# A wait ahead of the bursts of a row transform, five groups in flight in the next stage with six buffers, and a weight load in four pieces

## The chip, the cores and the metric

The kernel runs on one core of one Trainium2 chip. Its time is the device time of one execution in microseconds (us). The kernel before takes 1448.63 us, the median of three runs (1447.44 to 1449.13). The profile comes from one further execution of 1447.48 us, in which the span from the first to the last instruction is 1445.7 us.

## The reference

Two results over 2048 tokens with 576 channels are mixed by a gate per token.

```python
g = sigmoid((x * gate_w).sum(-1))
# a: a state-space layer as a long convolution
K = einsum("dn,dnl,dn->dl", C, exp(dt*A*l), dt*B).real      # 576 x 2048 taps from 128 states
y = irfft(rfft(u, 2L) * rfft(K, 2L))[:L] + u * Dskip
# b: a product-key mixture of 4096 single-neuron experts, 32 heads
q = einsum("nd,dhc->nhc", x, w_q)                           # two halves of 128 per head
s1, s2 = q1 . k1, q2 . k2                                   # 64 scores each; best 2 of each
top_s, top_e = best 2 of the 4 sums
out = sum over 64 picks of softmax(top_s) * gelu(x . u[e]) * v[e]
result = g * a + (1 - g) * b
```

The kernel computes x.u for all 4096 experts as a dense product, and the weighted sum of v as a dense product with a sparse matrix. Each number of a product is split into a high and a low 16-bit part, so that a product takes three passes.

## The kernel before, in words

**Who sets the order.** The kernel text is a planner. While it emits instructions it keeps a clock of its own, with assumed costs for each engine (classes `Engine`, function `mm`, `dma`), and runs some forty coroutines from a heap. A coroutine yields a time, or yields until a tile is due by that clock (`ready`), a bank of PSUM is free (`need`) or a slot is free. Whatever is emitted first stands first on its engine. So an edit of a few lines can move instructions on all engines behind it. The chip follows the order alone and waits by semaphores; the planner's times are not times of the chip.

**Row halves.** A matmul whose contraction has 64 rows uses one half of TensorE's rows. `rows` queues a product as 13 or 14 matmuls for the upper half and as many for the lower half; `row_slot` emits one matmul for each half in turn, out of `upper` (the queue of upper halves) and `lower`. While both are filled, the two halves work at the same time. `upper` is empty for a moment when one product's upper part has been emitted and the next is not yet begun.

**The stages.** In the first stage (to about 690 us) TensorE computes the scores (tiles `s`, weights `whl`/`wrem` folded from `wq` and the keys, tile `wb`) and the dense x.u (tiles `a`), both in row halves, and in between pieces of the convolution. The generator of the taps makes phases (`kP`), exponentials and sines, and a burst of 128 small matmuls for every second chunk (`kb`, 18 bursts); its coroutine `k_gen` already waits up to 6 planner us for `upper` to be empty. `u_stage1` transforms the input u in 16 rounds `p`; each has two bursts (`hh`) of six matmuls of 288 columns (tiles `u1_p_g_hh`, weights `tu`, data `uh`), and stores its result through `us` to DRAM. While such a round runs, `hungry` may be set, which keeps `k_front` from taking a bank for the next phases.

In the second stage, `k_stage1` transforms the taps: 32 groups `w` of eight matmuls of 288 columns (tiles `k1_w_hh`, data `ksb`) in row halves between the scores, each group in two banks of the set `wb` of four. ScalarE or VectorE copies a group into a buffer `k1o`, and SyncE's queue stores that to DRAM (`sk_d<-k1o`, 288 KB). `ring(n)` lets n groups be begun and not yet stored in the planner's account. In the same stretch `v_norm` loads the rows of u for the gate (`vn`, four transfers of 72 KB a tile); GpSimd multiplies and ScalarE sums them (`vj`). `w_next` loads the last weights of the scores, `wq`, 1152 KB for half of one of eight parts. Nearly all transfers are issued in order on SyncE's queue (SP).

In the third stage (`products`) the two spectra are multiplied and transformed back (`pr`, `pi`, `pv`). Then come one-hot matrices, the sparse matrix (`S`, `gl`, `wh`) and the last product with v (`o`), to the end.

Of the kernel before, what the change touches and what calls it, by code (L numbers as in the profile page):

```python
# [13 lines left out]
F32 = mybir.dt.float32  # L14
# [11 lines left out]
D = 576  # L26
# [6 lines left out]
NCK = 144 // NI  # L33
# [107 lines left out]
def body(ctx: ExitStack, tc: tile.TileContext, xT, au, par, logdt, dskip, gatew, wq, kT, uT, vv,  # L141
# [5 lines left out]
    clock = [0.0]  # L147
# [11 lines left out]
    def key(x):  # L159
        n = x.tensor.name  # L160
        return (n, x.offset) if n in columns else n

    def size(x):
        n = 1
        for d in x.shape[1:]:
            n *= d
        return n
# [34 lines left out]
    def dma(o, i, q=None):  # L202
        t = max(clock[0], rdy.get(key(i), 0.0), queue[0])
        queue[0] = t + 0.45
        wire[0] = max(wire[0], t) + (2 if o.dtype in (F16, BF16) else 4) * o.shape[0] * size(o) / 3.4e5
        rdy[key(o)] = max(rdy.get(key(o), 0.0), wire[0] + 2.2)
        (q or DQ).dma_start(o, i)
# [10 lines left out]
    upper, lower = deque(), []  # L218
# [71 lines left out]
    def ready(*xs, late=0.0):  # L290
        while True:
            t = max(rdy.get(key(x), 0.0) for x in xs) + late - clock[0]
            if t <= 0:
                return
            yield t
# [32 lines left out]
    def need(tag, n=1):  # L328
        while tag in banksets:
            lst = sorted(vacant)  # L330
            if held[tag] + n <= caps[tag] and len(lst) >= n and lst[n - 1][0] <= clock[0]:
                return
            yield max(0.2, min(0.3, lst[n - 1][0] - clock[0])) if len(lst) >= n else 0.3
        while True:
            lst = sorted(slots[tag])
            if len(lst) >= n and lst[n - 1] <= clock[0]:
                return
            yield max(0.2, lst[n - 1] - clock[0]) if len(lst) >= n else 0.3

    def take(tag, name):  # L340
        lst = slots[tag]
        assert lst, name
        lst.remove(min(lst))
# [52 lines left out]
    def pair_rows(x, n):  # L396

        return bass.AP(tensor=x.tensor, offset=x.offset + n * R1 * D, ap=[[D, R1], [32 * R1 * D, 4], [1, D]])
# [26 lines left out]
    def root_scale(bound2, margin, again=False):  # L425

        c, h, a, b = (newcol(again) for _ in range(4))
        V.tensor_scalar(sc[:, c], bound2, margin, 2.0 ** -120, op0=OP.mult, op1=OP.max)
        V.tensor_scalar(sci[:, h], sc[:, c].bitcast(I32), 24, 23, op0=OP.logical_shift_right, op1=OP.logical_shift_left)
        V.tensor_scalar(sci[:, a], sci[:, h], -1.0, float(204 << 23), op0=OP.mult, op1=OP.add)  # L430
        V.tensor_scalar(sci[:, b], sci[:, h], float(50 << 23), None, op0=OP.add)
        return sci[:, a].bitcast(F32), sci[:, b].bitcast(F32)
# [32 lines left out]
    def slot(shape, dt, name):  # L465
        take("slot", name)
        return bp.tile([128] + shape, dt, tag="s", name=name, bufs=9)
# [10 lines left out]
    def copy(o, i):  # L478
        copy2(((o, i),))
# [163 lines left out]
    whl, wl, sk, halves, scaled = {}, {}, [], {}, []  # L643
    side = lambda: "kb" if caps["wb"] == 0 else "wb"

    def w_load(c, h):
        a = slot([4, D], F32, f"wq{c}_{h}")
        g = 8 * c + 4 * h
        dma(a, wq[:, g:g + 4, :])
        wl[c, h] = a  # L650
# [94 lines left out]
    def w_next(c, h):  # L745
        while sdone[0] < c - (kdone[0] == NCK) and 8 * NT - len(groups) < NT * c - 5:
            yield 0.3
        yield from need("raw")
        take("raw", "raw")
        yield from need("slot")  # L750
        w_load(c, h)
        yield from w_half(c, h, wl[c, h])

    def w_build(c):
# [8 lines left out]
    kdone, kstored = [0], [0]  # L763
# [423 lines left out]
    def ring(n):  # L1187

        state = [0, set()]

        def enter():
            while state[0] - len(state[1]) >= n:
                yield 0.3
            state[0] += 1

        return enter, lambda k: state[1].add(k), lambda: len(state[1])

    def u_stage1():
        nonlocal uf
        yield from need("slot")  # L1200
        us = slot([4, D], F32, "us")
        columns.add(us.tensor.name)
        s_u, i_u = root_scale(nx2, 1.02)
        ended = [0]
        ld = {}

        def load(p):
            a = us[:, p % 2, :]
            for g in range(2):
                l, far = U_PAIRS[2 * p + g]  # L1210
                dma(a[64 * g:64 * g + 64], bass.AP(tensor=au.tensor, offset=au.offset + l * D,
                                                   ap=[[64 * D, R1], [(far - l) * D, 2], [1, D]]))
            tu = uf.tile([128, 2, 128], F16, tag="tu", name=f"tu{p}", bufs=2)
            dma(tu, tu_d[:, p])
            ld[p] = a, tu

        def tail(p, hh, tag, pbs):
            for g in range(2):
                o = us[:, 2 + g, :]
                pb = pbs[g]  # L1220
                yield from ready(pb)
                ov = o[:, 288 * hh:288 * hh + 288]
                S.activation(ov, pb[:, :288], AF.Copy)
                free(tag, ov, of=pb)
                if hh:
                    yield from ready(ov)
                    dma(pair_rows(su_d, 2 * p + g), o)
            ended[0] += hh

        load(0)  # L1230
        for p in range(NT):
            a, tu = ld.pop(p)
            yield from ready(a, tu)
            while ended[0] < p - 1:
                yield 0.3
            h = uf.tile([128, 2, D], F16, tag="uh", name=f"uh{p}", bufs=1)
            S.activation(h[:, 0], a, AF.Copy, scale=s_u)
            yield from ready(h)
            V.scalar_tensor_tensor(h[:, 1], a, s_u, h[:, 0], op0=OP.mult, op1=OP.subtract)
            if p + 1 < NT:  # L1240
                load(p + 1)
            yield from ready(h)
            while ended[0] < p:
                yield 0.3
            tag = side()
            hungry[0] = p * NCK < 17 * kdone[0]
            for hh in range(2):
                yield from need(tag, 2)
                pbs = [bank(tag, f"u1_{p}_{g}_{hh}") for g in range(2)]
                cs = slice(288 * hh, 288 * hh + 288)  # L1250
                for n, (z, w) in enumerate(((0, 0), (0, 1), (1, 0))):
                    for g in range(2):
                        r = slice(64 * g, 64 * g + 64)
                        mm(pbs[g][:, :288], tu[r, z], h[r, w, cs], n == 0, n == 2, 0.063)
                spawn(tail(p, hh, tag, pbs))
                del pbs
            hungry[0] = False
            yield 12
        while ended[0] < NT:
            yield 1  # L1260
        free("slot")
        quota(raw=2)
        while not kstored[0]:
            yield 1
        V.scalar_tensor_tensor(iuk, iuk, 2.0 ** -28, i_u, op0=OP.mult, op1=OP.mult)
        UF.__exit__(None, None, None)
        uf = 0

    def k_stage1(ksb, fk, tabs):
        enter, leave, count = ring(3)  # L1270

        def tail(w, o, pbs, gs):
            while not all(g["done"] for g in gs):
                yield 0.2
            yield from ready(*pbs)
            for hh in range(2):
                copy(o[:, 288 * hh:288 * hh + 288], pbs[hh][:, :288])
                free("wb", o, of=pbs[hh])
            yield from ready(o)
            dma(pair_rows(sk_d, w), o)  # L1280
            leave(w)

        for w in range(32):
            tkt = tabs[w // 16]
            yield from ready(tkt, ksb)
            yield from enter()
            o = fk.tile([128, D], F32, tag="s1o", name=f"k1o{w}", bufs=4)
            pbs, gs = [], []
            yield from need("wb", 2)
            for hh in range(2):  # L1290
                pb = bank("wb", f"k1_{w}_{hh}")
                pbs.append(pb)
                gs.append(rows(*([(pb[:, :288], tkt[h:h + 64, w % 16, n],
                                   ksb[h:h + 64, 2 * hh:2 * hh + 2, :, w, :].rearrange("p j c i -> p (j c) i"),
                                   h == 0 and n == 0, h == 64 and n == 1) for n in range(2)] for h in (0, 64)), first=True))
            spawn(tail(w, o, pbs, gs))
            del pb, pbs
        while count() < 32:
            yield 0.5
# [634 lines left out]
    while groups or acts:  # L1934
# [5 lines left out]
        a = choose(acts, a_fit)  # L1940
# [29 lines left out]
    for t in ORDER:  # L1970
        until(lambda: t in st)
        h = st.pop(t)
# [70 lines left out]
```

## Time and profile before

| what | us |
|---|---|
| median of three runs | 1448.63 |
| the profiled execution | 1447.48 |
| its span | 1445.7 |
| TensorE (PE) busy in the span | 1420.3 |
| VectorE (DVE) busy | 1199.7 |
| ScalarE (ACT) busy | 836.9 |
| GpSimd (POOL) busy | 470.1 |

The profile has a page with shares, a view by stretches of time, a view of who waited for whom, the chain of work that ended last, and the instructions in order of time. Busy time of PE counts a matmul in one row half as fully as two side by side. In the order of time, rows that follow each other with equal text are merged: the first number is the start, the second the length of the merged piece, and in brackets stands the idle time before it with what ended it.

### The profile page before, as it was taken

The page shows a single profiled execution, that of the slowest core. Times are in us where ns is not written, and L with a number is a line of the kernel's source. Part 1 is how long each engine was busy: PE and PEld are TensorE (multiplying, and loading weights), DVE is VectorE, ACT ScalarE, POOL GpSimd, SP SyncE. Part 2 cuts the span into 40 slices and gives each one's busy share as a digit, 9 for nine tenths or more (in the row PEclk, how much of TensorE's full clock was granted, in tenths as well). Part 3 has the DMA queues.
Part 4 walks back from the last instruction along what each step waited for, and adds up shares of the span by engine and source line. Part 5 has one row for each costly group of instructions (what it writes and reads, how often), then busy time and mean ns, then how long its engine had stood idle before and what let it go on. Part 6 is the DMA issues. An engine that isn't in the chain of part 4 may idle for free. (4 is left out here: it accounts for less than half of the span.)

```text
span 1445.7 us, 43987 instructions
## 1 busy us (share of the span) xinstructions
PE 1420.3 (98%) x17652; PEld 888.2 (61%) x17654; DVE 1199.7 (83%) x4611; ACT 836.9 (58%) x1454; POOL 470.1 (33%) x484
## 2 busy tenths in 40 slices
PE   7999999999999999999799999999999999999998
PEld 3465555554654654555565444446888888788887
DVE  5887687989988979789688998589989889889770
ACT  6547878778779688595576665655423322323230
POOL 0443273563553626631255899800000000000000
PEclk9999999999999999999999999999999999999999
DMA  9333543342351241236767689778334332531410
GB/s 316 118 109 98 170 135 121 93 141 84 114 173 67 76 122 46 86 114 221 225 226 248 230 283 325 248 236 280 120 120 126 129 120 76 178 121 68 137 59 17
DMA packets 134381, 215.89 MB, mean 149 GB/s; under 512 B 10913, under 2 KB 79905, under 8 KB 127777
## 3 DMA queue, kind: packets, MB, share of 16 engines
q1 hardware_dynamic: 134080, 213.01, 45.3%
q8 instruction: 138, 2.26, 0.7%
q14 instruction: 67, 0.54, 0.1%
q10 hardware_dynamic: 96, 0.07, 0.0%
HBM read 141.74 MB, written 71.30 MB: 147 GB/s over the span
## 5 line engine op out<-in xcount | busy, mean ns | idle before, releaser
L216 PE MATMUL s<-whl,xb 64*128 64x512 f16 x3072 | 478.7, 377 | 0.3 <-ACT k1o L136 0.3
L216 PE MATMUL a<-xb,uhl 64*128 64x512 f16 (+1 forms) x3024 | 470.0, 376 | 1.3 <-DVE CS L136 0.6
L216 PE MATMUL o<-vhl,wh 128*128 128x288 f16 x3072 | 387.3, 286 | 0.0
L216 PEld LDWEIGHTS <-wh 128*128 128x128 f16 x3072 | 295.8, 98 | 76.6 <-issue 4.1
L216 PEld LDWEIGHTS <-xb 64*128 64x128 f16 x3456 | 224.3, 94 | 178.4 <-issue 15.5
L216 PEld LDWEIGHTS <-uhl 64*128 64x128 f16 (+1 forms) x3024 | 194.6, 94 | 166.4 <-issue 10.0
L136 ACT ACTIVATE wh<-gl,s_wg 128x1024 f16<-128x1024 f32 x64 | 68.9, 1137 | 188.9 <-DVE gl L136 188.9
L136 POOL TENSOR_TENSOR CS<-CS,ex 128x512 f32<-128x512 f32 x72 | 91.7, 1306 | 161.6 <-DVE ex L136 145.2
L136 DVE FIND_INDEX8 i<-m,sx 128x8 uint32<-128x64 f32 x648 | 127.8, 218 | 0.0
L136 DVE TENSOR_TENSOR gl<-S,gl 128x256 f32<-128x256 f32 x256 | 90.7, 414 | 42.9 <-PE S L216 29.8
L216 PE MATMUL s<-wrem,xb 64*128 64x512 f16 x384 | 123.1, 376 | 0.0
L216 PE MATMUL a<-xb,wrem 64*128 64x512 f16 (+1 forms) x380 | 121.9, 376 | 0.0
L136 POOL TENSOR_TENSOR e<-aN,rt 128x512 f32<-128x512 f32 x72 | 84.0, 1186 | 62.2 <-PE kb L216 62.2
L136 ACT ACTIVATE gl<-gl 128x1024 f32<-128x1024 f32 x64 | 63.8, 1048 | 66.6 <-DMA gl<-g_d 66.6
L136 ACT ACTIVATE go<-a,i_a 128x512 f32<-128x512 f32 x100 | 68.1, 684 | 57.0 <-PE a L216 38.8
L136 DVE MAX8 m<-sx 128x8 f32<-128x64 f32 x648 | 89.2, 209 | 8.6 <-ACT sx L136 8.4
L136 DVE TENSOR_TENSOR Bg<-Be,vals 128x1024 f16<-128x1024 f16 x128 | 82.8, 688 | 2.2
L136 DVE SCALAR_TENSOR_TENSOR wh<-gl,s_wg,wh 128x1024 f16<-128x1024 f32 x64 | 78.9, 1277 | 1.0 <-ACT wh L136 0.9
L136 DVE TENSOR_TENSOR A<-iota_a,vals 128x2048 f16<-128x2048 f16 x64 | 77.7, 1214 | 0.0
L136 ACT ACTIVATE CS<-CS 128x1024 f32<-128x1024 f32 x69 | 71.2, 1050 | 9.5 <-DVE CS L136 9.3
L136 DVE FIND_INDEX8 i<-m,s 128x8 uint32<-128x64 f32 x376 | 75.7, 219 | 0.0
L216 PEld LDWEIGHTS <-A 128*128 128x128 f16 x2048 | 70.1, 97 | 5.7 <-issue 1.1
(208 smaller groups left out, 2355.9 us busy)
## 6 DMA issues: line engine op xcount, KB each, us to landing
g_d<-go SPq DMA_DIRECT2D x128, 256.0 KB, 2.7
gl<-g_d SPq DMA_DIRECT2D x32, 1024.0 KB, 6.7
wq<-in_wq_dram SPq DMA_DIRECT2D x16, 1152.0 KB, 6.2
su_d<-us SPq DMA_DIRECT2D x32, 288.0 KB, 2.6
sk_d<-k1o SPq DMA_DIRECT2D x32, 288.0 KB, 2.9
vn<-in_vv_dram SPq DMA_DIRECT2D x32, 288.0 KB, 4.8
ui<-su_d SPq DMA_DIRECT2D x16, 576.0 KB, 4.7
ki<-sk_d SPq DMA_DIRECT2D x16, 576.0 KB, 5.7
```

The lines of the kernel that those rows point to most:

```text
L136: return f(*a, **k)
L216: return T.matmul(o, l, r, start=start, stop=stop)
```

## The change

Three edits. `w_next` loads `wq` in one transfer while chunks of taps are still to be made, and afterwards in four of 288 KB, 2 planner us apart. `u_stage1` waits, ahead of each of its two bursts of a round, until `upper` is empty, though at most 2 planner us. `k_stage1` lets five groups be in flight, not three, and has six buffers `k1o`, not four.

```diff
@@ w_next
         yield from need("slot")
-        w_load(c, h)
+        a = wl[c, h] = slot([4, D], F32, f"wq{c}_{h}")
+        if kdone[0] < NCK:
+            dma(a, wq[:, 8 * c + 4 * h:8 * c + 4 * h + 4, :])
+        else:
+            for j in range(4):
+                dma(a[:, j], wq[:, 8 * c + 4 * h + j, :])
+                yield 2.0
         yield from w_half(c, h, wl[c, h])
@@ u_stage1
             hungry[0] = p * NCK < 17 * kdone[0]
             for hh in range(2):
+                end = clock[0] + 2
+                while upper and clock[0] < end:
+                    yield 0.1
                 yield from need(tag, 2)
@@ k_stage1
-        enter, leave, count = ring(3)
+        enter, leave, count = ring(5)
...
-            o = fk.tile([128, D], F32, tag="s1o", name=f"k1o{w}", bufs=4)
+            o = fk.tile([128, D], F32, tag="s1o", name=f"k1o{w}", bufs=6)
```

What this makes of the order is seen at two places. The first is TensorE at the first burst of round 11 of `u_stage1` (tiles `s2_8`, `s2_12`, `s2_13` are scores in row halves, `xb` their weights). Before:

```order
L216 LDWEIGHTS xb2_535
L216 MATMUL s2_8_6054<-whl2_4551,xb2_535 128x512
L216 LDWEIGHTS xb3_619
L216 MATMUL s2_12_6006<-whl2_4551,xb3_619 128x512
L216 LDWEIGHTS tu11_5519
L216 MATMUL u1_11_0_0_6076<-uh11_5805,tu11_5519 128x288
```

After:

```order
L216 LDWEIGHTS wb4_4954
L216 MATMUL kP17_1_6000<-rt_356,wb4_4954 128x512
L216 LDWEIGHTS xb3_619
L216 MATMUL s2_13_6004<-whl2_4437,xb3_619 128x512
L216 LDWEIGHTS xb3_619
L216 MATMUL s2_13_6004<-whl2_4437,xb3_619 128x512
```

Before, two products stand there in turn, one in each half. After, the burst has moved behind a row of twelve matmuls of one product, `s2_13`, all for the upper half, of which the first two are shown; ahead of `kP17_1` stand thirteen of another, `a3_2_0`, all for the lower half.

The second place is SyncE's queue in the middle of the second stage (`vn` are the rows for the gate). Before:

```order
L207 DMA sk_d_67<-k1o3_12163 32x4x576
L207 DMA wq7_0_12320<-in_wq_dram 128x2304
L207 DMA sk_d_67<-k1o6_12293 32x4x576
L207 DMA vn37_12386<-in_au_dram 32x576 x4
L207 DMA sk_d_67<-k1o5_12219 32x4x576
L207 DMA sk_d_67<-k1o7_12312 32x4x576
L207 DMA sk_d_67<-k1o8_12381 32x4x576
```

After:

```order
L207 DMA sk_d_67<-k1o13_12456 32x4x576
L207 DMA wq7_0_12613<-in_wq_dram 128x576
L207 DMA sk_d_67<-k1o15_12543 32x4x576
L207 DMA wq7_0_12613<-in_wq_dram 128x576
L207 DMA vn41_12676<-in_au_dram 32x576 x4
L207 DMA sk_d_67<-k1o16_12587 32x4x576
L207 DMA wq7_0_12613<-in_wq_dram 128x576
L207 DMA sk_d_67<-k1o17_12607 32x4x576
L207 DMA vn42_12769<-in_au_dram 32x576 x4
L207 DMA wq7_0_12613<-in_wq_dram 128x576
```

The one load of 1152 KB between the stores of groups 3 and 6 has become four loads of 288 KB between those of groups 13 and 18.

## The prediction

> **What bounds the kernel now.** First the page, for the shares:
>
> ```profile
> span 1445.7 us, 43987 instructions
> PE 1420.3 (98%) x17652; PEld 888.2 (61%) x17654; DVE 1199.7 (83%) x4611; ACT 836.9 (58%) x1454; POOL 470.1 (33%) x484
> ```
>
> TensorE (PE) is busy for 98% of the span. Then the view by stretches (length, busy time of PE, PEld, DVE, ACT, POOL, granted clock, DMA share, GB/s), cut at the stages, and the last step of the chain that ended last:
>
> ```profile
> 12.00:690.00 678.00, 675.10 (x8858) 367.76 (x8860) 577.01 (x2771) 508.96 (x830) 293.90 (x238) 1.00 0.40 125
> 697.00:720.50 23.50, 18.52 (x200) 13.02 (x199) 15.78 (x111) 14.67 (x44) 10.41 (x17) 1.00 0.58 183
> 720.50:727.30 6.80, 4.45 (x30) 3.20 (x31) 2.78 (x7) 3.11 (x7) 1.41 (x1) 0.50 0.90 309
> 727.30:785.00 57.70, 56.75 (x667) 36.04 (x667) 54.31 (x368) 40.18 (x117) 29.41 (x62) 1.00 0.68 223
> 785.00:942.00 157.00, 156.15 (x2040) 75.01 (x2034) 126.75 (x611) 95.12 (x262) 134.77 (x162) 1.00 0.79 271
> 942.00:1023.00 81.00, 80.97 (x934) 49.41 (x931) 77.22 (x126) 43.76 (x57) 0.00 (x0) 1.00 0.78 250
> 1023.00:1442.00 419.00, 418.93 (x4820) 338.70 (x4819) 337.71 (x563) 122.43 (x123) 0.00 (x0) 1.00 0.32 105
> 1397.96 44.11 PE o L216 x360
> ```
>
> PE has no idle time to speak of except between 697 and 727 us, the front of the taps' transform: 23.50 - 18.52 = 5.0 us idle, then 6.80 us at half clock of which 2.35 us idle. Behind 1023 us PE is the chain. In 942 to 1023 us the chain runs over DVE, but PE is as full (80.97 of 81.00). So I count in PE time: what is taken off PE's work or its idle time shortens the run, what is added lengthens it.
>
> Who PE waited for, in 12 to 690 us (the first two rows) and in 697 to 785 us (the rest; total, times, longest):
>
> ```profile
> PE u L216 <- DVE uh L136: 0.6, 1, 0.6
> PE u L216 <- DVE CS L136: 0.3, 1, 0.3
> PE k L216 <- DVE k1o L136: 5.0, 2, 4.1
> PE k L216 <- ACT k1o L136: 2.5, 2, 1.3
> PE k L216 <- DMA vn<-in_au_dram: 0.5, 1, 0.5
> PE s L216 <- ACT k1o L136: 0.3, 1, 0.3
> ```
>
> The second stage holds 8.3 us of waits, half of it one wait of 4.1. In order of time, on PE, DVE and SyncE's queue (SPq), with the two medians from issue to landing:
>
> ```profile
> 718.09 0.64 PE L216 MATMUL s<-whl,xb 64*128 64x512 f16 x3
> 722.85 0.39 PE L216 MATMUL k<-ksb,tk 64*128 64x288 f16 x1 [4.12 <-DVE k1o L136]
> 722.34 0.82 DVE L136 COPY k1o<-k 128x288 f32<-128x288 f32 x2 [6.71 <-DMA sk_d<-k1o]
> 711.47 1.95 SPq L207 DMA_DIRECT2D vn<-in_au_dram  x4
> 713.51 0.52 SPq L207 DMA_DIRECT2D sk_d<-k1o  x1
> 714.14 0.53 SPq L207 DMA_DIRECT2D wq<-in_wq_dram  x1
> 714.76 0.52 SPq L207 DMA_DIRECT2D sk_d<-k1o  x1
> 715.38 2.47 SPq L207 DMA_DIRECT2D vn<-in_au_dram  x4
> 717.95 2.93 SPq L207 DMA_DIRECT2D sk_d<-k1o  x3
> wq<-in_wq_dram SPq DMA_DIRECT2D x16, 1152.0 KB, 6.2
> sk_d<-k1o SPq DMA_DIRECT2D x32, 288.0 KB, 2.9
> ```
>
> At 714.14 the 1152 KB of `wq` are issued, and the stores of `k1o` come behind. DVE wants a buffer whose store has not landed and stands still for 6.71 us; nobody empties the banks; PE runs dry at 718.73 and goes on at 722.85. The clock falls to 0.50 from 720.5 to 727.3, so the work from 722.85 to 727.3 (4.45 us) takes twice its time: 2.2 us lost.
>
> **The change part by part.** *The stall.* With six buffers a copy needs the store of the sixth group back, not the fourth, and the 1152 KB no longer stand in one piece ahead of the stores. I take the wait away whole: -4.1 us, and with it the half clock, -2.2 us. The other waits of the stage (8.3 - 4.1 = 4.2 us) hang on banks and on ScalarE, which the change leaves: 0.
>
> *What comes late next.* The order now has a quick run, from group 13 to group 25. Between the stores of these two stand on SP 11 stores, 4 pieces of `wq` and 4 tiles `vn` of four transfers. From the starts above a store takes 714.76 to 715.38 = 0.62 us of the queue, `wq` as much, a tile `vn` 711.47 to 713.51 = 2.04: 11 x 0.62 + 4 x 0.62 + 4 x 2.04 = 17.5 us. On PE the same piece is 64 matmuls of 512 columns and 88 of 288, priced by these rows:
>
> ```profile
> 703.77 0.69 PE L216 MATMUL k<-ksb,tk 64*128 64x288 f16 x8
> 704.26 0.85 PE L216 MATMUL s<-whl,xb 64*128 64x512 f16 x6
> 974.63 2.11 PE L216 MATMUL a<-xb,uhl 64*128 64x512 f16 x18
> 976.57 0.38 PE L216 MATMUL a<-xb,wrem 64*128 64x512 f16 x1
> 129.00 0.81 PE L216 MATMUL a<-xb,uhl 64*128 64x512 f16 x3
> 129.65 0.59 PE L216 MATMUL a<-xb,wrem 64*128 64x512 f16 x2
> ```
>
> Eight of 288 in 0.49 us are 0.061 each; 18 of 512 in 1.94 us are 0.108 each, when both halves are filled. That makes 64 x 0.108 + 88 x 0.061 = 12.3 us, some 1.0 a group; with the pieces where one half is alone nearer 14, 1.15 a group. The queue falls 3.5 to 5.2 us behind by the end; a store needs 0.5 + 2.9 us more to land; the buffer comes round after six groups, 6.2 to 6.9 us. So a wait comes back of 0 (3.5 + 3.4 against 6.9) to 2.4 us (5.2 + 3.4 against 6.2). I take 1.0, nearer the low end, because some of these transfers can use the queue's gaps ahead of the run: +1.0.
>
> *The order of the row halves.* The last two rows above show a half alone: three matmuls from 129.00 to 129.65, 0.216 us each, twice the 0.108. Each matmul of 512 that runs alone so costs 0.108 us. I stepped through PE's two orders, put each matmul on its half, and counted, between changes of tile size, the columns for which the other half has nothing, in units of 512. If PE takes matmuls strictly in order there are 218 before and 272 now; if it may begin up to five ahead, fewer in both, and 42 to 49 more now. The new ones lie in the first stage: 12 and 11 around round 11 of `u_stage1`, and about 11 and 10 ahead of round 15. The wait alone does not make them: one half runs out when no product can be begun. So +4.5 (42 x 0.108) to +5.8 us (54); I take 48, +5.2.
>
> *The bursts of u.* The two waits at them, 0.6 and 0.3 us, may be covered by the added 2 us: between 0 and -0.9; I take -0.5. Behind the waiting coroutine stands the next round's load only; `k_front` is held longer by `hungry`, which is in the count above.
>
> *The pieces of `wq`.* Four halves (`wq6_0` to `wq7_1` in SP's order) are now four pieces each: 12 more issues of 0.62 us on SP, hidden where that queue has gaps, and counted above where it has not. The pieces land later than the whole did:
>
> ```profile
> vn<-in_vv_dram SPq DMA_DIRECT2D x32, 288.0 KB, 4.8
> ACT wj L136 <- DMA wq<-in_wq_dram: 1.3, 1, 1.3
> ```
>
> From the first piece to the last the queue issues three stores, two tiles `vn` and four pieces, 7.0 us or so; with 4.8 us to land (the like size from the like side) the half is there after 11.8 us instead of 6.2, 5.6 later. Only ScalarE waited for `wq` here, 1.3 us, and PE has other products: 0, with 5.6 as the far end. The Trainium skill speaks against this edit: "DMA: Bandwidth & Descriptors", section "Bandwidth", says to batch transfers to 1 MiB or more. By its fit in "Anatomy of one DMA" (2.0 us and the bytes at 436 GB/s, for the other issue path) the whole would take an estimated 4.7 us and four pieces one by one 10.7. The trace has 6.2 for the whole under load, and no piece of 288 KB of `wq`.
>
> **Sum**, against the profiled execution: 1447.48 - 4.1 - 2.2 + 1.0 + 5.2 - 0.5 = 1446.9 us. That execution lies 1.15 us below the median of the runs, so I say 1448.0 us: no difference that a measurement of this kernel tells from no change, which is about 0.2% or 2.9 us.
>
> **Rivals.** *The stall comes back in the quick run* (slower). The place is the copies of groups 24 and 25. The queue also stands still itself where a `vn` buffer is not free, and then the whole old price returns, 4.1 + 2.2 us instead of the 1.0: 1448.0 + 5.3 = 1453.3. It decides from about 2 us of further delay of the queue, since that makes a PE wait of 3 us and more, and the clock fell within 1.8 us of such a wait. For it speaks the 17.5 against 12.3 to 14 us; against it that the run is short and slow pieces follow.
>
> *All waits of the second stage go* (faster). Two of the other waits are banks that ScalarE empties late because it stands behind `vj`:
>
> ```profile
> ACT vj L136 <- POOL vn L136: 10.9, 7, 3.1
> ```
>
> In SP's order the load of `wq6_1`, which stood between the four parts of `ksb`, now stands behind them, so that `ksb`, `vn` and `vj` can come sooner. Then 4.2 and the 1.0 go as well: 1448.0 - 5.2 = 1442.8. Against it: the `vn` loads themselves are as before.
>
> *The split weights are late* (slower). If PE runs out of products before the last part of the scores, it waits up to the 5.6 us: 1453.6. By the page named above this is how it would go; the order has other products there, so I give it little.
>
> *The edit in `u_stage1` does not do what it says*: in round 11 the burst still stands beside an upper half, since 2 us ran out first. That is part of the likeliest case.
>
> **How the numbers follow.** No difference: 0.44. All waits go: 0.26. The stall comes back: 0.24; late weights: 0.06. So faster 0.26, same 0.44, slower 0.30. The likeliest case has its own range by the ends of its terms: 1447.48 - 6.3 + 0 + 4.5 - 0.9 + 1.15 = 1445.9 to 1447.48 - 6.3 + 2.4 + 5.8 - 0 + 1.15 = 1450.5. The range that is to hold 8 in 10 reaches to the other cases, 1442.8 to 1453.6.
>
> **What would show it.** The view of waits: no `PE k <- DVE k1o` over 2 us, and no half clock between 690 and 800 us. In 12 to 690 us, about 5 us more until the last `kb` for the same products, with rows like `s x11` that start 0.216 apart at round 11. A half clock in the second stage, or waits there over 6 us in sum, would speak for the slower rival; an `s` that waits for `whl` for the late weights. I would be wrong altogether if the order elsewhere brings new waits of more than 3 us, which I can't see from it.

## The result, and the profile after

The changed kernel takes 1455.51 us, the median of six runs (1454.69 to 1457.08), beside 1447.43 us for the kernel before on the same chip. The ratio is 1.0054 with the interval 1.0044 to 1.0064: half a per cent slower. Forecast were 1448.0 us and no difference, with a range that ended at 1453.6. The profiled execution is the quickest of the six, 1454.69 us.

The page of the kernel after, its first lines:

```profile
span 1452.9 us, 43977 instructions
PE 1428.6 (98%) x17652; PEld 890.6 (61%) x17654; DVE 1188.4 (82%) x4598; ACT 839.5 (58%) x1457; POOL 468.5 (32%) x484
```

TensorE (PE) has as many instructions as before, and is busy 8.3 us longer (1428.6 against 1420.3). The view by stretches of the kernel after:

```profile
12.00:690.00 678.00, 674.47 (x8694) 366.08 (x8696) 557.98 (x2642) 504.37 (x818) 291.60 (x238) 0.99 0.39 122
363.18:370.01 6.83, 6.77 (x34) 3.06 (x34) 6.22 (x9) 3.40 (x8) 5.58 (x5) 0.50 0.27 77
697.00:785.00 88.00, 80.31 (x997) 52.05 (x995) 76.31 (x525) 56.58 (x165) 39.31 (x75) 1.00 0.79 256
785.00:942.00 157.00, 156.94 (x2033) 75.68 (x2031) 130.56 (x701) 97.81 (x274) 137.35 (x168) 1.00 0.75 260
```

The last step of its chain:

```profile
1405.08 44.11 PE o L216 x360
```

The same stretch of the second stage in the kernel before:

```profile
697.00:785.00 88.00, 79.72 (x895) 52.26 (x897) 72.87 (x485) 57.96 (x168) 41.23 (x80) 0.96 0.67 219
```

Three things are to be read. In 12 to 690 us PE finishes 8694 matmuls where it finished 8858, though it is as busy (674.47 against 675.10): its work goes more slowly. (Of the 164 fewer, 81 are of 512 columns, 8.7 us at 0.108; most of the others are small ones, done later.) There is a new stretch at half clock in the first stage, 363.18 to 370.01 us. And the second stage has lost its half clock (1.00 against 0.96), but not its idle time: 88.00 - 80.31 = 7.69 us after, 88.00 - 79.72 = 8.28 before.

That gives the sum. The last row of the chain ends at 1405.08 + 44.11 = 1449.19 us, 7.1 us later than before (1442.07). Idle time of PE: first stage 3.53 after, 2.90 before, +0.6; second stage -0.6; third 0.06 against 0.85, -0.8. Half clock: half of the 6.77 us of busy time in it, 3.4, against 2.2 before, +1.2. What is left, 7.1 - 0.6 + 0.6 + 0.8 - 1.2 = 6.7 us, is work that went more slowly at full clock. I put it down to matmuls of one row half with nothing beside them; a difference that is left over doesn't show that by itself, so a count of them stands beside it further down.

Who PE waited for, in 12 to 690 us (first two rows) and in 697 to 785 us:

```profile
PE kP L216 <- DVE ko L136: 1.1, 1, 1.1
PE u L216 <- DVE CS L136: 0.3, 1, 0.3
PE k L216 <- DMA ksb<-k_d: 2.3, 1, 2.3
PE wn L216 <- ACT wj L136: 1.9, 3, 0.9
PE s L216 <- ACT k1o L136: 1.7, 2, 1.4
PE k L216 <- ACT sx L136: 1.0, 1, 1.0
```

The wait of 4.1 us on a copy of VectorE (DVE) is gone. In its place stand four that were not there or were shorter: on the data `ksb` at the front of the stage, on ScalarE's pieces of the weights (`wj`), on its copies `k1o` and on `sx`.

In order of time, PE at round 11 of `u_stage1`:

```profile
356.85 2.76 PE L216 MATMUL a<-xb,uhl 64*128 64x512 f16 x12
359.45 0.38 PE L216 MATMUL a<-xb,wrem 64*128 64x512 f16 x1
360.95 0.82 PE L216 MATMUL kP<-rt,wb 64*128 64x512 bf16 x2 [1.13 <-DVE ko L136]
361.39 3.16 PE L216 MATMUL s<-whl,xb 64*128 64x512 f16 x11
364.13 0.63 PE L216 MATMUL u<-uh,tu 64*128 64x288 f16 x2
```

Thirteen matmuls of one half run alone, 0.216 us each; PE stands still for 1.13 us; then eleven run alone for the other half. From 363.18 us the clock is 0.50. Waits of this length stand in the kernel before too (1.34 and 1.11 us in its second stage); what followed from this one is the surprise of the case.

### The profile page after: what moved, and what is told of

It is laid out like the page before. It is cut to its first block, busy times and chain, and to the rows that moved or that the text cites. A ratio compares the mean times of both kernels' runs of the same rounds, so it can differ in the third digit from the quotient of the medians.

```text
span 1452.9 us, 43977 instructions
## 1 busy us (share of the span) xinstructions
PE 1428.6 (98%) x17652; PEld 890.6 (61%) x17654; DVE 1188.4 (82%) x4598; ACT 839.5 (58%) x1457; POOL 468.5 (32%) x484
## 4 chain that ended last, share of the span: by engine, by line
PE 91%; DVE 3%; DMA 2%; SPq 1%; ACT 1%; issue 0%; POOL 0%; ACTq 0%; POOLq 0%; DVEq 0%
PE o L216 26%; PE a L216 26%; PE s L216 23%; PE S L216 4%; PE pr L216 2%; PE kb L216 2%; PE wb L216 2%; PE kP L216 2%; SPq L207 1%; PE pv L216 1%; PE y L216 1%; DVE i L136 1%; PE u L216 1%; DMA ksb<-k_d 1%; DVE e L136 1%; DVE m L136 1%
## 5 line engine op out<-in xcount | busy, mean ns | idle before, releaser
L216 PE MATMUL s<-whl,xb 64*128 64x512 f16 x3072 | 468.1, 378 | 1.9 <-ACT k1o L136 1.7
L216 PE MATMUL a<-xb,uhl 64*128 64x512 f16 (+1 forms) x3024 | 459.1, 376 | 0.5 <-DVE go L136 0.2
L216 PEld LDWEIGHTS <-xb 64*128 64x128 f16 x3456 | 219.0, 94 | 184.8 <-issue 17.2
L136 DVE FIND_INDEX8 i<-m,sx 128x8 uint32<-128x64 f32 x568 | 112.0, 218 | 0.0
L136 DVE FIND_INDEX8 i<-m,s 128x8 uint32<-128x64 f32 x456 | 91.9, 221 | 0.0
L136 DVE MAX8 m<-sx 128x8 f32<-128x64 f32 x568 | 78.2, 209 | 8.1 <-ACT sx L136 8.0
L136 DVE MAX8 m<-s 128x8 f32<-128x64 f32 x456 | 65.0, 214 | 12.2 <-PE s L216 8.8
```

What stands on the lines that cost most here:

```text
L136: return f(*a, **k)
L216: return T.matmul(o, l, r, start=start, stop=stop)
```

## The experiments

The prediction's theory was: the stall and its half clock go and nothing takes their place (-6.3 us), and the new order of the row halves costs 5.2. Fourteen kernels tell apart which edit does what, and why the clock fell. Ratios compare all runs with runs of the kernel before on the same chip. A profile is of one execution, and the executions of one kernel differ by some us: the profiled one was the quickest of eleven for the split load alone, the quickest but one for six buffers, and the slowest of four for the wait at u with five groups.

### Six buffers alone

```diff
-            o = fk.tile([128, D], F32, tag="s1o", name=f"k1o{w}", bufs=4)
+            o = fk.tile([128, D], F32, tag="s1o", name=f"k1o{w}", bufs=6)
```

> The kernel before with six buffers k1o instead of four and nothing else; the order of all engines is that of before. Theory 1 (the wait of 4.12 us and the half clock behind it hang on the buffers, and nothing takes their place): 4.1 + 2.2 = 6.3 us faster. Theory 2 (another wait of the second stage takes their place, as in the changed kernel, where that stage still has 7.7 us of waits): the 2.2 us of half clock go and under 1 us of idle time: 2 to 3 us faster.

1445.89 us, ratio 0.9988 (0.9979 to 0.9997). All engines keep the order of before, so nothing but the buffers differs. The median is 2.3 us under that of before. The second stage by the view of stretches:

```profile
697.00:785.00 88.00, 80.75 (x937) 51.03 (x933) 76.42 (x507) 58.63 (x171) 41.10 (x80) 1.00 0.72 234
```

PE's waits in it:

```profile
PE k L216 <- ACT k1o L136: 4.2, 3, 1.7
PE k L216 <- DVE k1o L136: 2.3, 2, 1.4
```

In order of time, DVE's copy behind the load of `wq`, and ScalarE some 13 us later:

```profile
722.54 0.82 DVE L136 COPY k1o<-k 128x288 f32<-128x288 f32 x2 [3.22 <-DMA sk_d<-k1o]
735.74 0.68 ACT L136 ACTIVATE vj<-vn 128x576 bf16<-128x576 f32 x1 [2.19 <-POOL vn L136]
```

DVE's wait for a store fell from 6.71 to 3.22 us, PE's wait there from 4.12 to 1.45, and no half clock follows. But PE's idle time fell by 1.0 us only, from 8.28 to 7.25. PE, which now comes to the next banks sooner, waits for them at 735.58 us, 1.72 us, where ScalarE stands behind `vj` and that behind GpSimd. Of the 6.3 us, some 2 arrived (1.7 by the ratio, 2.3 by the medians). The theory that nothing takes the stall's place has fallen.

### The split load alone

```diff
-        w_load(c, h)
+        a = wl[c, h] = slot([4, D], F32, f"wq{c}_{h}")
+        if kdone[0] < NCK:
+            dma(a, wq[:, 8 * c + 4 * h:8 * c + 4 * h + 4, :])
+        else:
+            for j in range(4):
+                dma(a[:, j], wq[:, 8 * c + 4 * h + j, :])
+                yield 2.0
```

> The weight load in four pieces alone. 210 matmuls run alone against 218 before: 0.9 us. Theory 1 (the load in one piece caused the stall): the 4.1 us wait and the half clock are gone, 5 to 7 us faster. Theory 2 (the pieces come late and PE waits at the sums of their squares, 1.9 us in the changed kernel): 2 to 4 us faster, with rows PE wn <- ACT wj.

1447.43 us, ratio 1.0000 (0.9991 to 1.0010). In the profiled execution the stall and the half clock are gone here too, and it takes 1445.61 us; over all eleven runs nothing is gained, where both theories had it faster. PE's longest waits on `k1o` are 1.3 us, but there are more of them, and at the end new ones on `Bg` of the one-hot matrices, 1.6 us. The view of transfers (count, size, median us from issue to landing) has for the pieces:

```profile
wq<-in_wq_dram SPq DMA_DIRECT2D x16, 288.0 KB, 3.9
```

A piece lands in 3.9 us, where the whole took 6.2, and less than the 4.8 that the prediction took from another transfer. The Trainium skill, "DMA: Bandwidth & Descriptors", section "Bandwidth", advises transfers of 1 MiB and more. Here the kernel with the pieces takes as long as the one without them.

### Three in pairs: both late edits, five groups alone, both with three groups in flight

The first is the changed kernel without the wait at the bursts of u:

```diff
             for hh in range(2):
-                end = clock[0] + 2
-                while upper and clock[0] < end:
-                    yield 0.1
                 yield from need(tag, 2)
```

> The changed kernel without the wait ahead of the bursts of u. Counted strictly in order 197 matmuls run alone, 21 fewer than before. Theory 1 (the loss is the u edit's): 21 x 0.108 = 2.3 us and some 2.8 us of the second stage: 4 to 7 us faster than before. Theory 2 (the second stage's edits lose as much by new waits as they take away): within 2 us of before or slower.

1445.40 us, ratio 0.9984 (0.9975 to 0.9993), the fastest of all, yet between the two theories. Even here the view of waits has a long one in the stage, and new ones in the third (`S`); the third row is ScalarE ahead of the copy that PE waits for, in order of time:

```profile
PE k L216 <- ACT k1o L136: 4.1, 2, 3.4
PE S L216 <- DVE Bg L136: 2.2, 4, 1.0
739.62 0.68 ACT L136 ACTIVATE vj<-vn 128x576 bf16<-128x576 f32 x1 [4.47 <-POOL vn L136]
```

The second is the kernel before with `ring(5)` and `bufs=6`, the load in one piece:

> Kernel before with five groups in flight and six buffers, the weight load in one piece, no wait at u. Theory 2: 1445 to 1447.5 us, as with six buffers alone or with the split load too; the 4.1 us wait is gone or halved and others of 1 to 2.5 us stand in its place. Rival (five in flight let PE run ahead of the stores, and the whole weight load stands in front of them): the stall comes back at over 3 us with a half clock, 1450 us.

1447.86 us, ratio 1.0003 (0.9994 to 1.0012). The longest wait is 3.2 us on a copy of DVE, which waits 3.51 us for a store: the rival's stall of over 3 us with a half clock behind it, but without a loss in the time. The third is the kernel before with the split load and `bufs=6`, but `ring(3)`:

> Kernel before with the split weight load and with six buffers, three groups in flight as before, no wait at u. Theory 2 (other waits take the place of the stall; they hang on banks that ScalarE empties, on ksb and on the weights): as with either edit alone, 1445 to 1447.5 us. Rival (the stores of k1o were what the waits hung on, and the two edits add): 1444 us or less, waits of the second stage under 5 us in sum.

1447.55 us, ratio 0.9997 (0.9988 to 1.0007), waits of over 6 us in sum (the longest `PE s` on ScalarE's `k1o`, 3.5). The rival, that the two edits add, has fallen. In each of the three, the clock falls for 3.41 us at the end of its long wait (at 741.21, 722.74 and 745.73 us), so part of the old loss is back. In the first and the third that wait is no matter of stores any more. ScalarE stands 4.47 and 4.34 us behind `vj`, for GpSimd's `vn`, and copies `k1o` after that; in the changed kernel it stands there for 2.88 us, with six buffers alone for 2.19. Whatever is done to the stores of `k1o` in this stage, 0.3 to 2.8 us come of it by the medians: another wait, mostly this one, then holds PE.

### The wait at the bursts of u alone

```diff
             for hh in range(2):
+                end = clock[0] + 2
+                while upper and clock[0] < end:
+                    yield 0.1
                 yield from need(tag, 2)
```

> The wait ahead of the bursts of u alone. Counted strictly in order there are 284 matmuls of 512 columns that run alone in a row half, against 218 before. Theory 1 (the loss is this edit's): 66 x 0.108 = 7.1 us, and the idle 1.1 us and half clock of 3.4 us at round 11 again: 10 to 12 us slower. Theory 2 (the loss comes of the second stage's edits): within 4 us of before.

1473.65 us, ratio 1.0179 (1.0165 to 1.0192): 25 us slower where 10 to 12 were expected, the loss of the changed kernel three times over. The first stage is that of the changed kernel, but for a half clock of 10.24 us in place of 6.83; the second has the old jam, larger. SyncE's queue, DVE, ScalarE and PE in order of time:

```profile
742.85 0.53 SPq L207 DMA_DIRECT2D wq<-in_wq_dram  x1
743.49 2.08 SPq L207 DMA_DIRECT2D sk_d<-k1o  x3
745.48 0.82 DVE L136 COPY k1o<-k 128x288 f32<-128x288 f32 x2 [2.81 <-DMA sk_d<-k1o]
753.66 1.41 ACT L136 ACTIVATE k1o<-k 128x288 f32<-128x288 f32 x4 [6.45 <-DMA sk_d<-k1o]
754.12 0.58 PE L216 MATMUL s<-whl,xb 64*128 64x512 f16 x1 [6.37 <-ACT k1o L136]
```

The half clock, which begins within that wait:

```profile
750.60:757.43 6.83, 3.31 (x22) 2.39 (x23) 2.25 (x16) 3.74 (x10) 1.35 (x4) 0.50 0.60 215
```

So the other two edits are no mere addition to this one: with the order that it makes, they save some 17 us; with the order of before, 2 to 3.

### The wait at u with five groups and six buffers

The changed kernel, with `w_load(c, h)` in one piece as before.

> Changed kernel without the split of the weight load: the wait at the bursts of u, and five groups with six buffers. The wait at u alone cost 25 us, of which 7 to 8 in the first stage, 13 in the second (one wait of 6.4 us behind the load of wq in one piece, with the half clock behind it) and 6 at the end. Theory 1 (the first stage's loss is the same in all kernels with this wait; the second stage's hangs on the stores of k1o behind wq and goes with six buffers): 1455 to 1460 us, first stage as in the changed kernel to 0.5 us, no wait over 3 us in the second stage. Theory 2 (the split load is what saves the second stage): 1465 us or more, with a wait over 4 us on a copy of k1o.

1460.86 us, ratio 1.0089 (1.0074 to 1.0105). The waits in the second stage:

```profile
PE k L216 <- ACT k1o L136: 3.1, 3, 1.9
PE wn L216 <- ACT wj L136: 2.5, 3, 0.9
```

That is theory 1 (1455 to 1460) but for 0.9 us: no wait over 3 us in this stage, and phases and rounds of u take 371.4 us (from the start of the first `kP` to that of the last `u`), as in the changed kernel. The clock falls twice more than there, at 756.58 and 927.25 us. `wn` waits for `wj` with the load in one piece as well, and longer (2.5 against 1.9), so those waits of the changed kernel are not due to the pieces.

### The wait at u, shorter and for one burst of the two

```diff
-                end = clock[0] + 2
+                end = clock[0] + 1
```

> Changed kernel, with the wait ahead of the bursts of u limited to 1 planner us instead of 2. Half the wait, yet in its order 108 to 132 more matmuls of 512 columns than in before have the other half empty (changed kernel: 48 to 54). Theory 1 (what the wait costs is the order of the row halves that follows from it, by chance of the planner's path): 11.7 to 14.3 us on top of the kernel with the two other edits alone (1445.4), so 1457 to 1460 us, slower than the changed kernel, and more with a fall of the clock. Theory 2 (the wait itself costs, by its length, through the late bursts): less than in the changed kernel, 1445 to 1455 us.

1477.28 us, ratio 1.0198 (1.0180 to 1.0215). With half the wait the loss is three and a half times that of the changed kernel (28.8 against 8.1 us), so theory 2 (by the wait's length) has fallen. But theory 1 was 17 us short. The waits of PE from 940 to 1025 us:

```profile
PE S L216 <- DVE Bg L136: 6.9, 4, 4.2
PE tr L216 <- ACT vals L136: 5.0, 1, 5.0
```

The first of two stretches at half clock, which begins within the wait of 5.0:

```profile
954.97:975.45 20.48, 16.35 (x148) 8.93 (x149) 10.99 (x26) 12.06 (x26) 0.00 (x0) 0.50 0.51 162
```

```diff
-                while upper and clock[0] < end:
+                while hh == 1 and upper and clock[0] < end:
```

> Changed kernel, with the wait ahead of the second burst of each round alone. Its order has 36 to 40 more matmuls of 512 columns with the other half empty than before. Theory 1 (the order of the row halves): 1445.4 + 3.9 to 4.3 = 1449.5 us, and 1453 if the clock falls at its one long lone run (13 matmuls ahead of phase kP13). Theory 2 (the waits' length): half the changed kernel's loss of 10 us against the kernel with the two other edits alone, 1450.5 us, with no fall of the clock. The time alone hardly tells them apart; the place of the loss does: by theory 1 the first stage is longer where the lone run stands.

1473.06 us, ratio 1.0166 (1.0151 to 1.0180), again far above the 1449.5 to 1453 expected. The lone run that was named, ahead of `kP13`, is in the trace, and the clock stays at 1.00 behind it:

```profile
320.68 2.75 PE L216 MATMUL a<-xb,uhl 64*128 64x512 f16 x12
324.20 0.82 PE L216 MATMUL kP<-rt,wb 64*128 64x512 bf16 x2 [0.55 <-DVE ko L136]
```

It falls in another lone run, which nobody had named, 1.93 us behind an idle time of 0.70 us (in order of time, and the stretch at half clock):

```profile
192.92 3.43 PE L216 MATMUL a<-xb,uhl 64*128 64x512 f16 x12 [0.70 <-DVE whl L136]
```

```profile
194.85:201.67 6.82, 6.76 (x31) 2.92 (x31) 4.96 (x7) 1.35 (x5) 6.29 (x5) 0.50 0.13 45
```

The rest of its loss is waits and half clocks that nobody had asked for, on `ksb` (3.6 us), `ui` (4.3) and `Bg` (8.2). I split each kernel's difference to before, up to the last matmul, in the way of the first section: idle time of PE from 20 us on, half of the busy time at clock 0.50, and what is left, in the profiled execution. Beside it stands the count of 512-column matmuls that have nothing in the other half, from the order as in the prediction (strict and with up to five ahead), times 0.108 us.

| kernel | idle | half clock | left | by the count |
|---|---|---|---|---|
| changed | -0.8 | +1.1 | +6.7 | 4.5 to 5.8 |
| six buffers | -1.3 | -2.2 | +1.0 | 0 |
| split load | +1.2 | -2.2 | -0.9 | -0.9 to -1.2 |
| both late edits | 0.0 | -0.5 | -1.8 | -1.5 to -2.3 |
| wait at u alone | +11.8 | +7.4 | +8.9 | 6.3 to 7.1 |
| u, five groups | +2.9 | +6.3 | +8.2 | 5.6 to 6.3 |
| u, second burst only | +9.8 | +13.1 | +3.3 | 3.6 to 3.9 |
| u, 1 us | +9.1 | +9.5 | +9.2 | 10.3 to 14.3 |
| lone halves (below) | +1.8 | +0.8 | +16.1 | 6.3 to 13.6 |

The count gives the last column but one to 2.5 us of its nearer end, and its rank but for the two highest. Six buffers alone, which keep the order of before, have +1.0 there, so a difference of 1 us says nothing. The count is no help with the first two columns, which are large in most kernels whose order the wait at u has disturbed, the other edits in it or not. What the wait at u costs is thus not given by its length; it follows the order that the planner falls into behind it.

### Does one row half alone let the clock fall?

At round 11 PE had been idle for 1.13 us only. In the kernel before, the clock fell within a wait of 4.12 us, and waits of 1.3 us did not let it fall. The first test has no wait at all. For 104 steps of the row queue the lower halves wait until no upper is left:

```diff
+    def alone():
+        return 1500 <= tick[0] < 1604
...
-        now = [g for g in lower if tick[0] - g["end"] > LAG or not upper]
+        now = [g for g in lower if tick[0] - g["end"] > LAG and not alone() or not upper]
...
-        if upper:
+        if upper or alone() and lower:
             row_slot()
             continue
```

> Kernel before, but for 104 steps of the row queue (between rounds 12 and 14 of u_stage1) a product's lower halves are emitted only when no upper half is left: some 54 matmuls of 512 columns then run alone in a row, 54 x 0.216 = 11.7 us, with no wait of PE asked for. The question is what made the clock fall at round 11 in the changed kernel, where 13 matmuls ran alone and PE then stood still for 1.13 us. Theory 1 (a low load is enough: rows in one half alone, without idle time): the granted clock falls to 0.50 in or just behind these 54 matmuls, for 6.8 us at least. Theory 2 (an idle wait is needed): the clock stays at 1.00 through them, and they take 0.216 us each. The order behind the place moves too; over the whole kernel 84 to 126 more matmuls of 512 columns have the other half empty than before, 9.1 to 13.6 us, so about 1457 to 1462 us without a fall of the clock and 3.4 us more for each fall.

1466.34 us, ratio 1.0123 (1.0108 to 1.0137), over the 1457 to 1462 expected without a fall; two half clocks of 3.41 us stand elsewhere, at 690.0 and 782.15 us. Two of the rows of one product's halves, in order of time:

```profile
394.81 2.77 PE L216 MATMUL a<-xb,uhl 64*128 64x512 f16 x14
400.23 2.33 PE L216 MATMUL a<-xb,uhl 64*128 64x512 f16 x10
```

The stretch around them:

```profile
394.80:404.80 10.00, 9.94 (x55) 4.28 (x53) 8.54 (x36) 9.94 (x13) 4.34 (x4) 1.00 0.35 106
```

The clock stays at 1.00, 55 matmuls in 10 us (at 0.216 us each, 46 would be one at a time throughout). A row half alone is not enough. Theory 1 has fallen; but theory 2, that an idle wait is needed, leaves open why 0.70 and 1.13 us were enough where 1.3 us were not. So I cut all traces into the stretches of 3.41 us by which the clock changes (the half clocks last 3.41, 6.83, 10.24 or 20.48 us) and summed what each feeds to the rows, as a share of what both halves can take: 0.216 us for a matmul of 512 columns in one half, counted half, since one half alone leaves the other empty. That suggested theory 3, and the next two kernels: 30 matmuls of one column, which feed nearly nothing, ahead of one product; once in the kernel with lone halves, once in the kernel before.

```diff
             o, l, r, start, stop = g["up"].popleft()
+            if start and tick[0] > 1530 and not thin:
+                thin.append(1)
+                for _ in range(30):
+                    T.matmul(o[:, :1], l, r[:, :1], start=True, stop=True)
```

> The kernel with the lone halves (some 54 matmuls of 512 columns in a row, one half at a time; clock 1.00 throughout), and in the midst of them, ahead of the third product, 30 matmuls of a single column (that feed the rows almost nothing, some 1.5 to 2 us; the bank is overwritten by the product behind them). The order is else the same. Read over all kernels so far, cut into stretches of 3.41 us that end where the clock changes, the clock fell after each stretch in which the rows were fed less than about 0.38 of what both halves can take, and, but for one, after none above 0.41. Theory 3 (that share decides, and one half alone counts as a half): 0.5 x (3.41 - 1.7) / 3.41 = 0.25 if the thin piece lies in one stretch, 0.37 if it is cut in the middle: the clock falls to 0.50 right behind it, and the kernel is 1.7 us and some 3 to 3.4 us slower than the one with lone halves (1466.3), 1471. Theory 4 (only a wait in which PE stands still counts): no fall, 1468.

> Kernel before, with the same 30 matmuls of a single column ahead of a product in the same stretch of the first stage, where both halves are filled on either side. Theory 3: the share is (3.41 - 1.7) / 3.41 = 0.50 at the least, so the clock stays at 1.00 there, and the kernel is 1.7 us slower than before, 1450. Theory 5 (any thin piece of this length lets the clock fall): a half clock at that place and 5 us more, 1453.

1466.32 and 1454.61 us (ratios 1.0128, 1.0113 to 1.0144, and 1.0037, 1.0024 to 1.0050). The dose was wrong, as the row of the 30 shows (the first and the last start, in us, behind the durations in ns):

```profile
L241 PE MATMUL s<-whl,xb x30: 160/160/173, 402.5 to 403.2; 64*128 64x1 f16 x30
```

They took 0.8 us, not 1.7, and the clock stayed at 1.00 in both: nothing told apart. The 6 us of the second kernel came later: its second stage, in the order of before, has falls of 6.8 and 10.2 us. Its ten runs show clocks of 0.994 to 0.999 and times from 1457.0 to 1449.0. The stretches are not tied to the kernel's start: taken from there, they begin 0.28 us behind a multiple of 3.413 us in the kernel before, 1.37 in the changed one and 3.10 with six buffers. So the same waits can let the clock fall more in one run than in the next; that this made the spread is likely, not shown. With 70 instead of 30:

```diff
-                for _ in range(30):
+                for _ in range(70):
```

> As the kernel with lone halves and 30 matmuls of one column in their midst, but with 70: the 30 took 0.027 us each, 0.8 us, half of what was meant, and the share there was 0.51 to 0.58 by the trace, so nothing was told apart. 70 take 1.9 us. Theory 3 (the share of the rows fed in a stretch of 3.41 us decides, one half alone counts as a half, the bound near 0.38): 0.5 x (3.41 - 1.9) / 3.41 = 0.22 in one stretch, 0.36 if cut in the middle (a little more where a product's end overlaps the next one's start): the clock falls to 0.50 just behind the 70. Theory 4 (only a wait in which PE stands still counts): clock 1.00 there.

> As the kernel before with 30 matmuls of one column between products that fill both halves, but with 70. Theory 3: the share is (3.41 - 1.9) / 3.41 = 0.44 if they lie in one stretch, 0.72 if cut in the middle: clock 1.00 there. Theory 5 (any thin piece of 1.9 us lets the clock fall): 0.50 just behind it.

1476.96 us (1.0182, 1.0155 to 1.0209) and 1448.85 us (1.0008, 0.9997 to 1.0019). Among lone halves, PE in order of time:

```profile
401.62 2.33 PE L216 MATMUL a<-xb,uhl 64*128 64x512 f16 x10
404.22 1.54 PE L241 MATMUL s<-whl,xb 64*128 64x1 f16 x45
405.62 3.73 PE L216 MATMUL s<-whl,xb 64*128 64x512 f16 x12
```

By stretches:

```profile
403.82:407.24 3.42, 3.37 (x79) 2.40 (x74) 2.15 (x6) 3.42 (x5) 3.42 (x4) 1.00 0.10 29
407.24:417.48 10.24, 10.18 (x114) 4.90 (x115) 0.62 (x2) 3.26 (x6) 2.08 (x2) 0.50 0.23 81
```

Among full halves, in order of time and by stretches:

```profile
406.23 1.84 PE L238 MATMUL a<-xb,uhl 64*128 64x1 f16 x68
```

```profile
404.71:408.12 3.41, 3.41 (x88) 2.52 (x86) 3.41 (x22) 3.34 (x7) 1.80 (x2) 1.00 0.80 256
408.12:411.54 3.42, 3.42 (x34) 2.34 (x32) 1.17 (x4) 1.99 (x6) 0.00 (x0) 1.00 0.82 260
```

In the first PE counts as busy all the time (3.37 of 3.42 us, no wait), and the clock falls to 0.50 right behind, for 10.24 us. In the second the same 70, in one stretch, leave it at 1.00. By the sums the shares of the two stretches are 0.33 and 0.50. So theory 4 (only standing still counts) and theory 5 (any thin piece) have both fallen, each by one execution, and theory 3 stands: what the rows are fed in a stretch decides, and a lone half counts as a half. Over the sixteen traces (30 to 1390 us) there are 29 falls. By the sums 25 of them follow a share of 0 to 0.39; the other four follow stretches with small tiles of other kinds (`wn`, `kb`, `pv`), for which the sums are not sure. Of some 5,460 stretches at full clock without a fall the lowest have 0.38 (the lone run ahead of `kP13` with the wait of 0.55 us), 0.41 and 0.41, so the bound lies near 0.4 and is not sharper than that. Round 11 of the changed kernel has 0.33: 1.13 us of idle time and the rest at half.

The Trainium skill, "TensorE: Matmul & The Clock Gate", section "Part 1: The HAM clock gate (the "warmup" mystery)", gives the free-running window of 3413 ns; the traces agree (3.41 us and multiples). Its rule that an idle window of some 3.4 us brings the half clock fits three of the 29 falls (share 0, in waits of 3.44, 3.52 and 4.21 us), but the clock fell without such a window too: after 1.13 us of idle time, after 0.70 us, and with none at all.

## Why the prediction was wrong

**The stall, -4.1, and the half clock behind it, -2.2.** Both are gone from their place, as said. The step that failed is "hang on banks and on ScalarE, which the change leaves: 0", said of the other waits of the stage. The change does not leave them. With six buffers alone PE comes to the next banks sooner and waits there for longer (on ScalarE's copies 4.2 us in sum, 2.5 before); in the changed kernel waits on `ksb` (2.3) and `wj` (1.9) have taken the place. The stage's idle time went from 8.28 to 7.69 us, -0.6 where -3.1 was summed (-4.1 + 1.0). Six buffers alone show it without any change of order: the stall fell by 2.7 us, the idle time by 1.0. The new wait on the banks hangs on ScalarE behind `vj`, that is on GpSimd's `vn`; the prediction had that row, as the ground of its faster rival.

**The half clock as a term at all.** I wrote of it only as what follows the stall. A second step failed here: the rise of lone halves was priced at 0.108 us each and its effect on the clock not at all. Round 11, which I had named as the place of the new lone halves, then fell to half clock: +3.4 us, and the wait on `ko` there +1.1. The clock term came to +1.2 in place of -2.2, the largest single part of the miss. By the test with the thin piece this is no accident of that place: a lone stretch leaves the share at 0.5, and a wait of 0.8 us in 3.41 brings it to 0.38. It is no certainty either, as the lone run ahead of `kP13` shows.

**The order of the row halves, +5.2.** The mechanism is borne out by the count over nine kernels. The place is too: the 81 fewer matmuls of 512 columns are 8.7 us, and less the half clock and the waits there (3.4 and 0.6) some 4.7 us are left for the first stage. 6.7 us are left for it in the sum, over its range of 4.5 to 5.8 by no more than the split is good for.

**The bursts of u, -0.5.** Two waits of 0.6 and 0.3 us became one of 0.3: nearly as said. "The edit does not do what it says" at round 11 was right too, and beside the point, since the cost came from the order.

**The quick run, +1.0 (0 to 2.4).** No wait of that kind: no copy of a `k1o` waits for a store in the stage after the change.

**The pieces of `wq`, 0.** Right: the split alone has the ratio 1.0000, and the waits of `wn` on `wj` are there without it.

**The rivals.** "The stall comes back" gave a time 2.2 us under the measured one, by a mechanism that did not occur. "All waits go" did not occur: the runs show that in this stage most of a wait taken away comes back at another place. "The split weights are late" did not occur either: no `s` waits for `whl` in the stage. The sum with what was measured is 1447.48 - 0.8 (idle time) + 1.2 (clock) + 6.7 (order) = 1454.6, where the profiled execution of the kernel after took 1454.69. It closes because the 6.7 is what was left over; with the 4.5 to 5.8 of the count it gives 1452.4 to 1453.7. The sentence "I would be wrong altogether if the order elsewhere brings new waits of more than 3 us" did not name the right danger. The new waits elsewhere are small, and it was the clock that made one of them dear.

## What to carry to other kernels

A stall with other waits close behind it can be worth much less than its length: here some 2 us of 6.3 by six buffers alone, nothing by the split load alone, and 2 to 3 by all the late edits together. A few lines in a planner that sets the order are priced by the order they lead to, on which other edits then gain or lose another sum (some 17 us against 2 to 3). And where row halves run alone, a short wait is dearer than it looks: count, by stretches of 3.41 us, what the rows are fed, and keep it over 0.4 of what both halves can take.

## What the runs showed of the hardware

The granted clock follows what the rows are fed, not whether TensorE is busy. It fell to 0.50 for 10.24 us behind a stretch in which PE was busy 3.37 of 3.42 us with lone halves and one-column matmuls, and stayed at 1.00 through 10 us of lone halves (share over 0.5) and behind the same 70 one-column matmuls among full halves. And a matmul of one column takes 0.025 us from start to start (30 started within 0.74 us, 70 among full halves within 1.73; among lone halves 0.029), weights loaded for each, where its row shows 0.16 us from start to end.
